# Attention on one core: the exponentials on VectorE as three half-float bit patterns, and 70 rows of them in place of 51

## The chip, the cores and the metric

The kernel runs on one core of one Trainium2 chip. Its time is the device time of one execution in microseconds. The profile is one execution, taken instruction by instruction; its span reaches from the first to the last instruction. TensorE does the matmuls, VectorE (DVE), ScalarE (ACT) and GpSimd (POOL) the elementwise work, SyncE (SP) issues most transfers.

## The reference

One multi-head attention layer with 16 heads of 28 columns, over 2048 positions of 448 columns, in bfloat16:

```python
qkv = (x @ wqkv).reshape(B, S, 3, H, Dh).transpose(2, 0, 3, 1, 4)   # B 1, S 2048, H 16, Dh 28
q, k, v = qkv
scores = einsum("bhqd,bhkd->bhqk", q, k) * Dh ** -0.5
o = einsum("bhqk,bhkd->bhqd", softmax(scores, -1), v)
return o.transpose(0, 2, 1, 3).reshape(B, S, D) @ wo
```

There are 16 × 2048 × 2048 = 67 million exponentials.

## The kernel before

**Units, rows and tiles.** The heads form four groups of four. A unit is one head group with one chunk of 512 queries: 16 units, counted from 0, four to a group (unit 12 is the first of the last group). A unit has 16 rows, one for each block of 128 keys, and a row has four tiles, one for each head: scores of 128 keys by 512 queries, one PSUM bank each. There are 256 rows and 1024 tiles. Rows are numbered through, so row 196 is row 4 of unit 12.

**Two ways to the exponentials.** Most rows go to ScalarE. A score group (`S`, line 864) puts two or three tiles into neighbouring banks of the five banks 0 to 4, and one activation (line 939) writes their exponentials to slots of `PT`, 36 slots of one tile each. Other rows, 51 of them, go to VectorE. Each of their tiles is computed alone (`SD`, also line 864), mostly beside a score group, in one of the `M` banks (5 to 7). Since the queries are scaled by 128 · log2(e), one instruction (line 886: a maximum and an addition) turns a score into the integer whose bits are about the bfloat16 number 2^z. When all four tiles stand in `DY`, four more instructions over the whole row (lines 896 to 902) make a power of two, `DS`, and a correction, `DU`. There are three buffers of each.

**Products with V.** TensorE multiplies the exponentials with V (`PV`, line 832), four heads side by side, into one `M` bank for a unit, in the order of the rows. Only a row's product frees its slots. A VectorE row needs three products: `DY` and `DS` with `V`, `DU` with `VK`, a weighted copy of V that GpSimd makes (line 577). A column of ones in V gives the sums for the softmax. At a unit's end VectorE copies the result out (line 731), the sums go through DRAM to be spread over the partitions (`scr_l`, `LT`, `scr_r`, `RB`, on SP's queue), and VectorE normalises (line 747). Units 12 to 15 finish the four query chunks, and behind each of them stand four output tiles: four matmuls each (line 718), one copy on VectorE (line 706) and one store. For the last unit the parts that don't need it (line 766) come ahead.

**What sets the order.** The transposes of x and the projections of Q, K and V stand among the units; those of later groups, and the output tiles, also need an `M` bank. A list scheduler with costs for each instruction fixes the order on every engine when the program is built. A planner chooses the VectorE rows ahead of it: it adds `rcost` to VectorE's account for each such row and `acost` to ScalarE's for each tile, and leaves at least `rgap` rows between two. `dlead` is how many tiles ahead of its place a row may start. Where the scheduler counts too little activity of TensorE, it puts in passes that multiply zeros (line 469).

```python
if t_d + CFG["rcost"] <= t_a + CFG["rlead"] and r < NROW - CFG["rend"] and gap >= CFG["rgap"]:
    t_d = max(t_d, t_a - 6.0) + CFG["rcost"]
    rows.append(r)
```

Of the kernel before, what the change touches and what calls it, by code (L numbers as in the profile page):

```python
# [334 lines left out]
CFG = {"late": 4.5, "load": 1.5, "load0": 18, "dcost": 2.3, "dlead": 32, "aslack": 250, "opp": 0.0, "oload": 2.5, "klead": 0.5, "vlag": 0.04, "hot1": 45000.0, "hotm": 3600.0, "nslack": 1300.0, "dlook": 20.0, "plook": 362.5, "rcost": 5.6, "rlead": 1.0, "rend": 4, "rgap": 2, "acost": 0.4455, "dprio": 0.0, "nride": 2}  # L335

PLAN = {
    "rows": None,
# [4 lines left out]
def _fast(nc, x, wqkv, wo, out, n_heads=16):  # L343
# [20 lines left out]
    QSCALE = 128.0 * LOG2E * scale  # L364
    ESCALE = 1.0 / (128.0 * LOG2E)
# [9 lines left out]
    P = _Prog()  # L375
    es = ExitStack()
    with es:
        def sb(name, shape, dt):
            return es.enter_context(nc.sbuf_tensor(name, shape, dt))
# [11 lines left out]
        VK = sb("VK", [128, NK, HC], BF16)  # L391
        DY = sb("DY", [128, NDR, 2048], I16)
        DS = sb("DS", [128, NDR, 2048], I16)
        DU = sb("DU", [128, NDR, 2048], FP16)
# [162 lines left out]
        v_ev = {}  # L557
        vk_ev = {}

        def proj_v(g, c, prio, early):  # L560
            mms = []
            for j in range(4):
                n = 4 * c + j

                def f(e, b, j=j, n=n):
                    ins = None
                    for it in range(NIT):
                        ins = e.matmul(ps[:, b * 512 + j * GD:b * 512 + (j + 1) * GD], xT[0:IT, it, n * 128:(n + 1) * 128],  # L568
                                       w_raw[0:IT, it, 2 * D + g * GD:2 * D + (g + 1) * GD], start=(it == 0), stop=(it == NIT - 1))
# [5 lines left out]
            vs = V[:, 4 * c:4 * c + 4, g * 128:(g + 1) * 128]  # L575
            vd = VK[:, 4 * c:4 * c + 4, g * 128:(g + 1) * 128]
            vk_ev[(g, c)] = P.add("pool", (lambda e: e.tensor_scalar(vd, vs, KAP, 1.0, ALU.mult, ALU.mult)), deps=[v_ev[(g, c)]],  # L577
                                  dur=1500, prio=prio, name=f"vk_{g}_{c}")


        for c in range(NCH):
# [231 lines left out]
        def pv(u, kt):  # L813
            g, c = units[u]
            r = u * NK + kt
            if r in n_row:
                ri = n_row[r] % NDR
                terms = [(V, DY[:, ri, :].bitcast(BF16)), (V, DS[:, ri, :].bitcast(BF16)), (VK, DU[:, ri, :].bitcast(BF16))]
                parts = [(w_, [t_[:, h * 512:(h + 1) * 512] for h in range(4)]) for w_, t_ in terms]
                deps_of = [row_ops[r], [row_ev[r][0]], [row_ev[r][1], vk_ev[(g, kt // 4)]]]  # L820
                slots = []
            else:
                slots = [tile_slot[(u, kt, h)] for h in range(4)]
                parts = [(V, [PT[:, pi * 512:(pi + 1) * 512] for _, pi in slots])]
                deps_of = [list({id(tile_ev[(u, kt, h)]): tile_ev[(u, kt, h)] for h in range(4)}.values())]

            def f_pv(e, k, w_, p_):
                ins = None
                b = pv_open[u].banks[0]
                for h in range(4):  # L830
                    hh = 4 * g + h
                    ins = e.matmul(ps[32 * h:32 * h + 32, b * 512:(b + 1) * 512], w_[:, kt, hh * 32:(hh + 1) * 32],  # L832
                                   p_[h], start=(kt == 0 and k == 0), stop=(kt == NK - 1 and k == len(parts) - 1), tile_position=(0, 32 * h))
# [12 lines left out]
            if r in n_row:  # L846
                row_pv[n_row[r]] = op
            if kt == NK - 1:
                (last_unit if u == NU - 1 else post_unit)(u, op)

        last_pv = [None]
# [19 lines left out]
        def row_tile(r, h, ph, partner, p_pr):  # L871
            u, kt = r // NK, r % NK
            g, c = units[u]
            t = (u, kt, h)
            if r not in n_row:
                n_row[r] = len(n_row)
                row_ops[r] = []
            ri = n_row[r] % NDR
            old = row_pv.get(n_row[r] - NDR)
            assert n_row[r] < NDR or old is not None, "DVE rows too close"  # L880
            deps = [kq_ev[(0, g, c)], kq_ev[(1, g, kt // 4)]] + (early_ev if ph > 0 else []) + (mid_ev if ph == 2 else [])
            hold = []
# [3 lines left out]
            o1 = P.add("dve", (lambda e, ri=ri, h=h, s=s: e.tensor_scalar(DY[:, ri, h * 512:(h + 1) * 512], bank(s.banks[0]), ZLO, ZADD, ALU.max, ALU.add)),  # L886
                       deps=[s, old], dur=600, prio=-90.0, name=f"D1_{r}_{h}", rel=[(s, 0)])
# [7 lines left out]
            Gt = U.bitcast(I16)  # L895
            og = P.add("dve", (lambda e: e.tensor_scalar(Gt, Y, 0x7F, 0x3F80, ALU.bitwise_and, ALU.bitwise_or)),  # L896
                       deps=row_ops[r] + [old], dur=600, prio=pr, name=f"DG_{r}")
            os_ = P.add("dve", (lambda e: e.tensor_scalar(S_, Y, 0xFF80, None, ALU.bitwise_and)),  # L898
                        deps=row_ops[r] + [old], dur=600, prio=pr + 0.001, name=f"DS_{r}")
            ou = P.add("dve", (lambda e: e.tensor_tensor(U, Gt.bitcast(BF16), Gt.bitcast(BF16), ALU.mult)),  # L900
                       deps=[og], dur=1130, prio=pr + 0.002, name=f"DU_{r}")
            oa = P.add("dve", (lambda e: e.tensor_tensor(U.bitcast(BF16), Y.bitcast(BF16), U, ALU.mult)),  # L902
                       deps=[ou], dur=1130, prio=pr + 0.003, name=f"DA_{r}")
            row_ev[r] = [os_, oa]
            done.update(4 * r + j for j in range(4))

# [815 lines left out]
```

## Time and profile before

| | |
|---|---|
| device time, three runs | 398.53, 403.58 and 403.67 us, median 403.58 |
| span of the profiled execution | 406.7 us (no other time of this execution is shown) |
| busy: TensorE, ScalarE, VectorE, GpSimd | 386.9, 378.0, 371.8 and 16.8 us |
| mean granted TensorE clock | 0.970 of full speed |
| matmuls; of these with zeros | 4331; 928 |
| ScalarE's exponentials (line 939) | 335 instructions, 375.0 us |
| VectorE's rows (lines 886 and 896 to 902) | 204 and 4 × 51 instructions |

A line of a group gives the source line, the engine, the operation, the output and inputs by the program's names, their shapes and the count; then busy time in us, the mean of one in ns, the idle time of the engine just ahead of them, and what ended most of it. PEld is TensorE's loading of weights. Instructions of one engine may overlap a little, so a group's busy time can be less than its count times its mean.

### The profile page before, as it was taken

How to read it: one execution, taken by the hardware profiler on the slowest of the kernel's cores; microseconds unless marked ns; L12 is line 12 of the kernel's file. 1: busy time of each engine (PE TensorE's matmuls, PEld its weight loads, DVE VectorE, ACT ScalarE, POOL GpSimd, SP SyncE). 2: the span in 40 equal slices, each digit the busy share in tenths (PEclk: the TensorE clock that was granted, in tenths of full speed). 3: DMA queues.
4: the chain of work that ended last, by engine and by line, in shares of the span. 5: the costliest groups of instructions: out<-in, count | busy, mean ns of one | idle time of the engine just before them, and what ended most of it. 6: DMA issues, size and time to landing. Idle time of an engine off the chain costs nothing.

```text
span 406.7 us, 9742 instructions
## 1 busy us (share of the span) xinstructions
PE 386.9 (95%) x4331; PEld 123.9 (30%) x4331; DVE 371.8 (91%) x548; ACT 378.0 (93%) x339; POOL 16.8 (4%) x25
## 2 busy tenths in 40 slices
PE   8999999999999999999999899999999899999997
PEld 4433323322323332333322222222222212222223
DVE  6569978999999999999999999999999967899964
ACT  2999979999999999999999999999999967999983
POOL 3010000200001000020000000000000000000000
PEclk9999969999999999999999999999999957999999
DMA  8200000000000000000000000000000000110111
GB/s 259 81 2 2 13 19 3 29 0 19 12 3 29 3 28 2 23 8 4 29 1 30 5 26 6 4 27 2 27 3 29 2 23 6 36 38 14 41 59 59
DMA packets 12980, 10.26 MB, mean 25 GB/s; under 512 B 5064, under 2 KB 10952, under 8 KB 12932
## 3 DMA queue, kind: packets, MB, share of 16 engines
q1 hardware_dynamic: 12132, 8.92, 7.1%
q8 instruction: 35, 0.57, 0.6%
q10 hardware_dynamic: 800, 0.66, 0.5%
q14 instruction: 13, 0.11, 0.1%
HBM read 7.50 MB, written 2.08 MB: 24 GB/s over the span
## 4 chain that ended last, share of the span: by engine, by line
ACT 43%; DVE 34%; PE 19%; DMA 2%; issue 1%; SPq 0%
ACT PT L939 43%; DVE DY L886 11%; PE ps L864 7%; DVE DU L900 6%; DVE DU L902 5%; PE ps L832 5%; DVE DU L896 3%; DVE DS L898 3%; PE ps L469 3%; PE ps L718 2%; DMA LT<-scr_l 2%; PE ps L550 2%; DVE V L521 1%; DVE KT L521 1%; DVE QT L519 1%; DVE OTS L731 1%
## 5 line engine op out<-in xcount | busy, mean ns | idle before, releaser
L939 ACT ACTIVATE PT<-ps 128x1536 bf16<-128x1536 f32 (+1 forms) x335 | 375.0, 1317 | 14.6 <-PE ps L864 13.9
L864 PE MATMUL ps<-QT,KT 28*128 28x512 bf16 x1024 | 164.2, 393 | 12.6 <-ACT PT L939 8.4
L886 DVE TENSOR_SCALAR DY<-ps 128x512 int16<-128x512 f32 x204 | 132.7, 679 | 11.0 <-PE ps L864 10.8
L864 PEld LDWEIGHTS ps<-QT,KT 28*128 28x128 bf16 x1024 | 40.3, 91 | 153.8 <-ACT PT L939 101.1
L832 PE MATMUL ps<-PT,V 128*32 128x512 bf16 x820 | 80.2, 398 | 2.1 <-issue 1.2
L469 PE MATMUL ps<-ZM,ZW 128*32 128x512 bf16 x928 | 74.9, 399 | 1.2 <-DVE ZM L451 1.2
L902 DVE TENSOR_TENSOR DU<-DY,DU 128x2048 bf16<-128x2048 bf16 x51 | 61.9, 1213 | 0.1
L900 DVE TENSOR_TENSOR DU<-DU 128x2048 f16<-128x2048 bf16 x51 | 61.8, 1213 | 0.0
L896 DVE TENSOR_SCALAR DU<-DY 128x2048 int16<-128x2048 int16 x51 | 34.7, 680 | 0.3
L550 PE MATMUL ps<-xT,w_raw 112*32 112x512 bf16 x512 | 35.0, 388 | 0.0
L898 DVE TENSOR_SCALAR DS<-DY 128x2048 int16<-128x2048 int16 x51 | 34.6, 678 | 0.0
L832 PEld LDWEIGHTS ps<-PT,V 128*32 128x32 bf16 x820 | 19.7, 94 | 47.1 <-issue 41.1
L469 PEld LDWEIGHTS ps<-ZM,ZW 128*32 128x32 bf16 x928 | 21.1, 98 | 27.9 <-issue 18.0
L832 PE MATMUL ps<-DU,VK 128*32 128x512 bf16 x204 | 20.8, 397 | 0.0
L832 PE MATMUL ps<-DY,V 128*32 128x512 bf16 x204 | 20.8, 397 | 0.0
L832 PE MATMUL ps<-DS,V 128*32 128x512 bf16 x204 | 20.6, 394 | 0.0
L577 POOL TENSOR_SCALAR VK<-V 128x512 bf16<-128x512 bf16 x16 | 13.4, 837 | 171.6 <-DVE V L521 171.6
L568 PE MATMUL ps<-w_raw,xT 112*128 112x112 bf16 x256 | 16.6, 214 | 0.0
L550 PEld LDWEIGHTS ps<-xT,w_raw 112*32 112x32 bf16 x512 | 12.0, 97 | 13.6 <-issue 3.0
L521 DVE CAST KT<-ps 128x512 bf16<-128x512 f32 x16 | 10.9, 682 | 4.4 <-PE ps L550 4.4
L568 PEld LDWEIGHTS ps<-w_raw,xT 112*128 112x128 bf16 x256 | 13.0, 98 | 5.8 <-issue 4.7
L706 DVE CAST OUTS<-ps 128x448 bf16<-128x448 f32 x14 | 8.6, 620 | 5.0 <-PE ps L864 2.6
(50 smaller groups left out, 121.2 us busy)
## 6 DMA issues: line engine op xcount, KB each, us to landing
RB<-scr_r SPq DMA_DIRECT2D x15, 256.0 KB
out_dram<-OUTS SPq DMA_DIRECT2D x14, 112.0 KB, 1.7
XO<-in_x_dram SPq DMA_DIRECT2D x3, 448.0 KB, 6.8
w_raw<-in_wqkv_dram SPq DMA_DIRECT2D x2, 392.0 KB, 6.5
wop<-in_wo_dram SPq DMA_DIRECT2D x16, 24.5 KB
scr_l<-OTS SPq DMA_DIRECT2D x15, 8.0 KB
LT<-scr_l SPq DMA_DIRECT2D x15, 8.0 KB, 1.6
scr_r<-RS SPq DMA_DIRECT2D x15, 8.0 KB, 1.4
```

Source lines behind the costliest of these rows:

```text
L469: ins = e.matmul(ps[32 * h:32 * h + 32, b * 512:(b + 1) * 512], ZW[:, :], ZM[:, :], start=shut, stop=shut, skip_group_check=not shut, tile ...
L521: fe = (lambda e: e.tensor_copy(evac[0](), evac[1](hold[0].banks[0])))
L550: ins = e.matmul(ps[32 * h:32 * h + 32, b * 512:(b + 1) * 512], w_raw[0:IT, it, col:col + 32], xT[0:IT, it, c * 512:(c + 1) * 512], start= ...
L568: ins = e.matmul(ps[:, b * 512 + j * GD:b * 512 + (j + 1) * GD], xT[0:IT, it, n * 128:(n + 1) * 128], w_raw[0:IT, it, 2 * D + g * GD:2 * D ...
L832: ins = e.matmul(ps[32 * h:32 * h + 32, b * 512:(b + 1) * 512], w_[:, kt, hh * 32:(hh + 1) * 32], p_[h], start=(kt == 0 and k == 0), stop= ...
L864: ins = e.matmul(bank(b), KT[32 * h:32 * h + rows, g, kt * 128:(kt + 1) * 128], QT[32 * h:32 * h + rows, g, c * QCH:(c + 1) * QCH], start= ...
L886: o1 = P.add("dve", (lambda e, ri=ri, h=h, s=s: e.tensor_scalar(DY[:, ri, h * 512:(h + 1) * 512], bank(s.banks[0]), ZLO, ZADD, ALU.max, AL ...
L896: og = P.add("dve", (lambda e: e.tensor_scalar(Gt, Y, 0x7F, 0x3F80, ALU.bitwise_and, ALU.bitwise_or)), deps=row_ops[r] + [old], dur=600, p ...
L898: os_ = P.add("dve", (lambda e: e.tensor_scalar(S_, Y, 0xFF80, None, ALU.bitwise_and)), deps=row_ops[r] + [old], dur=600, prio=pr + 0.001, ...
L900: ou = P.add("dve", (lambda e: e.tensor_tensor(U, Gt.bitcast(BF16), Gt.bitcast(BF16), ALU.mult)), deps=[og], dur=1130, prio=pr + 0.002, na ...
L902: oa = P.add("dve", (lambda e: e.tensor_tensor(U.bitcast(BF16), Y.bitcast(BF16), U, ALU.mult)), deps=[ou], dur=1130, prio=pr + 0.003, name ...
L939: ex = P.add("act", (lambda e, p0=p0, w=w, bf=bf: e.activation(PT[:, p0 * 512:(p0 + w) * 512], bank(bf(), w), AF.Exp, scale=ESCALE)), deps ...
```

## The change

The bit pattern becomes that of a half-float: queries are scaled by 1024 · log2(e), and the integer in `DY` is read as a half-float. The two other terms are the same integer plus 342 and plus 683, a third and two thirds of 1024, which moves z by 1/3 and 2/3. Each is multiplied with its own weighted copy of V (0.793 and 0.629). So `DS` and `DU` take one integer addition each in place of four instructions for a row. The copies, `VK1` and `VK2`, hold two head groups and are made on VectorE: for group 0 after each chunk of V, for the others once, after the last chunk, and for groups 2 and 3 after the last product of the group two before. `PT` has 30 slots, not 36; the row buffers are four, not three; `rcost` is 3.6, not 5.6, and `dlead` 24, not 32. With that the planner picks 70 rows.

```diff
-KAP = 0.1669921875
-ZLO = -64.0 * 128.0
-ZADD = 127.0 * 128.0 - 128.0 * 1.115731919743946
+HB = 1024.0
+SH1, SH2 = 342, 683
+KAP1, KAP2 = 0.79296875, 0.62890625
+ZADD = HB * (15.0 - 1.6415719559093558)
+ZLO = -ZADD
...
-    NPT = 36
-    NDR = 3
+    NPT = 30
+    NDR = 4
...
-            vk_ev[(g, c)] = P.add("pool", (lambda e: e.tensor_scalar(vd, vs, KAP, 1.0, ALU.mult, ALU.mult)), deps=[v_ev[(g, c)]],
-                                  dur=1500, prio=prio, name=f"vk_{g}_{c}")
+            if g == 0 or c == NCH - 1:
...
+                    op = P.add("dve", (lambda e, vd=vd, vs=vs, w_=w_: e.tensor_scalar(vd, vs, w_, None, ALU.mult)), deps=evs,
...
-                terms = [(V, DY[:, ri, :].bitcast(BF16)), (V, DS[:, ri, :].bitcast(BF16)), (VK, DU[:, ri, :].bitcast(BF16))]
+                terms = [(None, DY[:, ri, :].bitcast(FP16)), (VK1, DS[:, ri, :].bitcast(FP16)), (VK2, DU[:, ri, :].bitcast(FP16))]
...
+                        if g_ == g + 2 and op not in o_.deps:
+                            o_.deps.append(op)
...
-            og = P.add("dve", (lambda e: e.tensor_scalar(Gt, Y, 0x7F, 0x3F80, ALU.bitwise_and, ALU.bitwise_or)),
-            os_ = P.add("dve", (lambda e: e.tensor_scalar(S_, Y, 0xFF80, None, ALU.bitwise_and)),
-            ou = P.add("dve", (lambda e: e.tensor_tensor(U, Gt.bitcast(BF16), Gt.bitcast(BF16), ALU.mult)),
-            oa = P.add("dve", (lambda e: e.tensor_tensor(U.bitcast(BF16), Y.bitcast(BF16), U, ALU.mult)),
+            os_ = P.add("dve", (lambda e: e.tensor_scalar(S_, Y, SH1, None, ALU.add)),
+            oa = P.add("dve", (lambda e: e.tensor_scalar(U, Y, SH2, None, ALU.add)),
```

The lines of the changed program stand some places lower: the exponentials are at 947, scores at 877, tiles to integers at 899, the two additions at 908 and 910, products with V at 841, zeros at 472, copies of V at 584, projections at 553 and 571, output tiles at 727 and 775.

First place: VectorE around the tiles of unit 2, where rows follow each other. Before, the work of one row (line 886 to 902) with three tiles of the next among it and, at L731 and L521, other copies:

```order
L886 TENSOR_SCALAR DY<-ps 128x512 x4
L896 TENSOR_SCALAR DU<-DY 128x2048
L886 TENSOR_SCALAR DY<-ps 128x512
L898 TENSOR_SCALAR DS<-DY 128x2048
L886 TENSOR_SCALAR DY<-ps 128x512 x2
L731 COPY OTS<-ps 128x512
L886 TENSOR_SCALAR DY<-ps 128x512
L900 TENSOR_TENSOR DU<-DU 128x2048
L521 CAST V<-ps 128x4x4x28
L902 TENSOR_TENSOR DU<-DY,DU 128x2048
```

And after:

```order
L899 TENSOR_SCALAR DY<-ps 128x512 x2
L908 TENSOR_SCALAR DS<-DY 128x2048
L899 TENSOR_SCALAR DY<-ps 128x512 x2
L910 TENSOR_SCALAR DU<-DY 128x2048
L899 TENSOR_SCALAR DY<-ps 128x512 x2
L740 COPY OTS<-ps 128x512
L908 TENSOR_SCALAR DS<-DY 128x2048
L910 TENSOR_SCALAR DU<-DY 128x2048
```

Between two rows' tiles stand two instructions over 128x2048, not four, and none of them is a product of two tiles.

Second place: TensorE at the start of unit 12, around the first VectorE row of that unit. Before, V's projections have long been done, and the three products of the row (`DY`, `DS`, `DU`) stand together:

```order
L864 MATMUL ps<-QT,KT 128x512 x5
L832 MATMUL ps<-PT,V 32x512 x4
L864 MATMUL ps<-QT,KT 128x512 x2
L832 MATMUL ps<-DY,V 32x512 x4
L832 MATMUL ps<-DS,V 32x512 x4
L832 MATMUL ps<-DU,VK 32x512 x4
L469 MATMUL ps<-ZM,ZW 32x512 x4
```

After, the last projections of K (553) and V (571) stand between the row's first and second product, with zeros where a product could have stood:

```order
L841 MATMUL ps<-DY,V 32x512 x4
L877 MATMUL ps<-QT,KT 128x512 x5
...
L877 MATMUL ps<-QT,KT 128x512
L553 MATMUL ps<-xT,w_raw 32x512 x16
L877 MATMUL ps<-QT,KT 128x512 x5
L571 MATMUL ps<-w_raw,xT 128x112 x16
L877 MATMUL ps<-QT,KT 128x512 x4
L472 MATMUL ps<-ZM,ZW 32x512 x4
L877 MATMUL ps<-QT,KT 128x512 x3
L472 MATMUL ps<-ZM,ZW 32x512 x8
L841 MATMUL ps<-DS,VK 32x512 x4
```

The second product moved behind the copies of the whole group's V, and eight score groups lie between the two.

Third place: TensorE behind the last score group (the last row of line 864 or 877), up to the sums of the last unit (785; 794). Before:

```order
L864 MATMUL ps<-QT,KT 128x512 x2
L832 MATMUL ps<-PT,V 32x512 x12
L766 MATMUL ps<-wop,XO 128x448 x2
L832 MATMUL ps<-PT,V 32x512 x4
L766 MATMUL ps<-wop,XO 128x448 x3
L785 MATMUL ps<-SEL,OTS 128x4 x4
```

After, the first and the last rows of a longer stretch:

```order
L877 MATMUL ps<-QT,KT 128x512 x4
L841 MATMUL ps<-DS,VK 32x512 x4
L841 MATMUL ps<-DU,VK 32x512 x4
L841 MATMUL ps<-PT,V 32x512 x4
L727 MATMUL ps<-wop,XO 128x448 x4
L841 MATMUL ps<-PT,V 32x512 x4
L775 MATMUL ps<-wop,XO 128x448 x6
L727 MATMUL ps<-wop,XO 128x448 x2
...
L841 MATMUL ps<-DU,VK 32x512 x4
L841 MATMUL ps<-PT,V 32x512 x20
L794 MATMUL ps<-SEL,OTS 128x4 x4
```

Twelve of the last unit's sixteen rows now have products behind the last score group, and so have four output tiles.

More of the change, by code (lines that the diff above doesn't have):

```diff
@@ L390, in _fast @@
         PT = sb("PT", [128, NPT * 512], BF16)
-        VK = sb("VK", [128, NK, HC], BF16)
+        VK1 = sb("VK1", [128, 2, NK, 128], BF16)
+        VK2 = sb("VK2", [128, 2, NK, 128], BF16)
         DY = sb("DY", [128, NDR, 2048], I16)
         DS = sb("DS", [128, NDR, 2048], I16)
-        DU = sb("DU", [128, NDR, 2048], FP16)
+        DU = sb("DU", [128, NDR, 2048], I16)
         OTS = sb("OTS", [128, 2, 512], FP32)
@@ L574, in proj_v @@
                                ((lambda: Vd), (lambda b: bank(b)[:, 0:4 * GD].rearrange("p (n h d) -> p n h d", n=4, d=DH)), ms_v1), early, evac_dur=600)
[L575 to L578 removed]
+            if g == 0 or c == NCH - 1:
+                n0 = 4 * c if g == 0 else 0
+                vs = V[:, n0:4 * c + 4, g * 128:(g + 1) * 128]
+                evs = [v_ev[(g, cc)] for cc in range(n0 // 4, c + 1)]
+                for k_, (VK_, w_) in enumerate(((VK1, KAP1), (VK2, KAP2))):
+                    vd = VK_[:, g % 2, n0:4 * c + 4, :]
+                    op = P.add("dve", (lambda e, vd=vd, vs=vs, w_=w_: e.tensor_scalar(vd, vs, w_, None, ALU.mult)), deps=evs,
+                               dur=200 if g == 0 else 600, prio=prio + 0.01, name=f"vk{k_}_{g}_{c}")
+                    for cc in range(n0 // 4, c + 1):
+                        vk_ev[(g, cc, k_)] = op
         for c in range(NCH):
@@ L817, in pv @@
                 ri = n_row[r] % NDR
-                terms = [(V, DY[:, ri, :].bitcast(BF16)), (V, DS[:, ri, :].bitcast(BF16)), (VK, DU[:, ri, :].bitcast(BF16))]
-                parts = [(w_, [t_[:, h * 512:(h + 1) * 512] for h in range(4)]) for w_, t_ in terms]
-                deps_of = [row_ops[r], [row_ev[r][0]], [row_ev[r][1], vk_ev[(g, kt // 4)]]]
+                terms = [(None, DY[:, ri, :].bitcast(FP16)), (VK1, DS[:, ri, :].bitcast(FP16)), (VK2, DU[:, ri, :].bitcast(FP16))]
+                parts = [((lambda h, w_=w_: V[:, kt, (4 * g + h) * 32:(4 * g + h + 1) * 32] if w_ is None else w_[:, g % 2, kt, h * 32:(h + 1) * 32]),
+                          [t_[:, h * 512:(h + 1) * 512] for h in range(4)]) for w_, t_ in terms]
+                deps_of = [row_ops[r], [row_ev[r][0], vk_ev[(g, kt // 4, 0)]], [row_ev[r][1], vk_ev[(g, kt // 4, 1)]]]
                 slots = []
@@ L823, in pv @@
                 slots = [tile_slot[(u, kt, h)] for h in range(4)]
-                parts = [(V, [PT[:, pi * 512:(pi + 1) * 512] for _, pi in slots])]
+                parts = [((lambda h: V[:, kt, (4 * g + h) * 32:(4 * g + h + 1) * 32]), [PT[:, pi * 512:(pi + 1) * 512] for _, pi in slots])]
                 deps_of = [list({id(tile_ev[(u, kt, h)]): tile_ev[(u, kt, h)] for h in range(4)}.values())]
@@ L848, in pv @@
             if kt == NK - 1:
+                if c == NCH - 1:
+                    for (g_, _, _), o_ in vk_ev.items():
+                        if g_ == g + 2 and op not in o_.deps:
+                            o_.deps.append(op)
                 (last_unit if u == NU - 1 else post_unit)(u, op)
```

16 lines of the change are left out of this document (6 added, 10 removed).

## Prediction

> **What bounds the kernel now.** I read the busy row first, then the groups, then the idle time of ScalarE in order of time, and last the windows in which the TensorE clock fell.
>
> ```profile
> span 406.7 us, 9742 instructions
> PE 386.9 (95%) x4331; PEld 123.9 (30%) x4331; DVE 371.8 (91%) x548; ACT 378.0 (93%) x339; POOL 16.8 (4%) x25
> ACT 43%; DVE 34%; PE 19%; DMA 2%; issue 1%; SPq 0%
> L939 ACT ACTIVATE PT<-ps 128x1536 bf16<-128x1536 f32 (+1 forms) x335 | 375.0, 1317 | 14.6 <-PE ps L864 13.9
> L469 PE MATMUL ps<-ZM,ZW 128*32 128x512 bf16 x928 | 74.9, 399 | 1.2 <-DVE ZM L451 1.2
> ```
>
> ScalarE has one kind of work, the exponentials of L939, and it is idle for only 14.6 us between them, 13.9 of these for the score matmuls of L864. VectorE is as full (371.8 us). The chain that ended last swaps between the two. TensorE's 95% is no third bound: 928 of its matmuls multiply zeros (L469) and are put in only to keep it active. So an exponential taken off ScalarE brings time only if VectorE takes it at a lower price than now.
>
> Where ScalarE starts, runs gaplessly and ends (start, length, count):
>
> ```profile
> 9.82 25.77 ACT L939 ACTIVATE PT<-ps 128x1024 bf16<-128x1024 f32 x28 [0.63 <-PE ps L864]
> 232.23 92.77 ACT L939 ACTIVATE PT<-ps 128x1536 bf16<-128x1536 f32 x82 [0.31 <-PE ps L864]
> 335.99 2.53 ACT L939 ACTIVATE PT<-ps 128x1536 bf16<-128x1536 f32 x2 [0.91 <-PE ps L864]
> 340.28 15.92 ACT L939 ACTIVATE PT<-ps 128x1536 bf16<-128x1536 f32 x14 [1.76 <-PE ps L864]
> 391.93 6.95 ACT L939 ACTIVATE PT<-ps 128x1536 bf16<-128x1536 f32 x7 [1.12 <-PE ps L864]
> ```
>
> 28 exponentials of two banks take 25.77 us, 0.920 each. The 82 in the middle are three and two banks in turn: 41 pairs of 2.263, so three banks take 1.343. The last ends at 398.9, which leaves 7.8 us to the end of the span. Much of the idle time lies where the granted clock was half (columns: window, its length, then PE, PEld, DVE, ACT and POOL busy, PEclk):
>
> ```profile
> 51.00:57.80 6.80, 6.80 (x53) 1.25 (x45) 4.38 (x7) 4.87 (x5) 0.00 (x0) 0.50 0.07 26
> 232.00:324.00 92.00, 85.77 (x1031) 23.91 (x1028) 91.59 (x130) 91.77 (x82) 0.00 (x0) 1.00 0.05 14
> 324.00:341.00 17.00, 16.87 (x114) 3.42 (x118) 11.72 (x16) 11.39 (x11) 0.00 (x0) 0.50 0.06 18
> ```
>
> At full clock ScalarE works 91.77 of 92 us; at half clock it idles 5.6 of 17.0 (the waits of 0.91 and 1.76 for scores are among them) and 1.9 of 6.8: 7.5 us in all. That fits the runs: the profiled execution (406.7) lies 3.1 over the median of 403.6 and 8.2 over the fastest, 398.5. I make the sum against 406.7 and take 3.1 off at the end, which assumes that the clock falls about as often as now.
>
> **The change, part by part.** *ScalarE.* 19 more rows of 4 tiles leave it, 76 of 820 tiles. From the order of both programs: 152 groups of three banks become 137, 181 of two become 166, two single ones become one. At the durations above that is 371.9 before (the row says 375.0) and 337.4 after: **−34.5 us**, to about 340.5.
>
> *VectorE.* Its rows:
>
> ```profile
> L886 DVE TENSOR_SCALAR DY<-ps 128x512 int16<-128x512 f32 x204 | 132.7, 679 | 11.0 <-PE ps L864 10.8
> L902 DVE TENSOR_TENSOR DU<-DY,DU 128x2048 bf16<-128x2048 bf16 x51 | 61.9, 1213 | 0.1
> L900 DVE TENSOR_TENSOR DU<-DU 128x2048 f16<-128x2048 bf16 x51 | 61.8, 1213 | 0.0
> L896 DVE TENSOR_SCALAR DU<-DY 128x2048 int16<-128x2048 int16 x51 | 34.7, 680 | 0.3
> L898 DVE TENSOR_SCALAR DS<-DY 128x2048 int16<-128x2048 int16 x51 | 34.6, 678 | 0.0
> 153.14 1.28 DVE L886 TENSOR_SCALAR DY<-ps 128x512 int16<-128x512 f32 x2
> ```
>
> Neighbours overlap by 0.08 us: two L886 take 1.28, so the second adds 0.60 beside a duration of 0.68. Taken so, a row costs now 4 × 0.60 + 2 × 0.60 + 2 × 1.13 = 5.86, and afterwards, if an int16 addition costs what the int16 masks of L896 and L898 cost, 6 × 0.60 = 3.60. That is 51 × 5.86 = 299 against 70 × 3.60 = 252, −47. The weighted copies of V come from GpSimd to VectorE: six over 128x2048 at 0.60, and eight over 128x512, which no row shows on VectorE; between a quarter of that (0.15) and L886 (0.60) I take 0.3, and get +6. VectorE falls to 371.8 − 47 + 6 = 331: below ScalarE, so its saving is no gain of its own. The removed GpSimd copies had cover:
>
> ```profile
> L577 POOL TENSOR_SCALAR VK<-V 128x512 bf16<-128x512 bf16 x16 | 13.4, 837 | 171.6 <-DVE V L521 171.6
> ```
>
> An engine that waits 171.6 us and works 13.4 sets nothing; I count 0. But the copies now wait for the whole V of their head group. In unit 12 the second term of row 2 stands eight score groups behind the first, with every later product of the unit behind it; meanwhile ScalarE fills some 20 of the 30 slots in 8 × 1.13 = 9 us and is not held. In the order, all exponential groups but two of the last three find the products that free their slots issued before the next score group; so fewer slots (30 for 36), four buffers for three and the later start of rows cost 0 up to the end.
>
> The addition itself is the one unknown that matters. Same tiles, types and shape as L898, other arithmetic: the low end is 0.60; nothing makes it cheaper. The high end is one element at a time: L886 does 512 in about 0.53 beyond its fixed part, so 2048 take about 2.2. I take 0.60, by the nearest row.
>
> The Trainium skill speaks against it: "Advanced Engine Details and Errata", section "VectorE Performance Modes", lists BF16 and FP16 for the packed mode and not int16. By that sentence an int16 operation would get two elements a cycle, 1.13 us. This case's trace disagrees for the masks: int16 in 680 ns, against 1213 for the two-input product. The sum goes by the trace.
>
> *TensorE.* A pass (up to four matmuls side by side) follows a like one after 0.22 us; going between scores and anything else costs 0.1 more:
>
> ```profile
> 393.97 0.93 PE L718 MATMUL ps<-wop,XO 128*128 128x448 bf16 x4
> 394.83 0.39 PE L864 MATMUL ps<-QT,KT 28*128 28x512 bf16 x2
> 395.15 0.40 PE L832 MATMUL ps<-PT,V 128*32 128x512 bf16 x4
> 395.38 0.39 PE L832 MATMUL ps<-DY,V 128*32 128x512 bf16 x4
> 395.70 0.39 PE L864 MATMUL ps<-QT,KT 28*128 28x512 bf16 x3
> ```
>
> (395.15 to 395.38; 394.83 to 395.15. Four L718 and the switch take 0.86: 0.19 each.) Counted in the orders: score passes 419 then 472, since more single tiles of rows no longer ride beside a group; products with V 358 then 396; projections 128 and 144 small groups unchanged; switches 656 then 630. Useful TensorE time: 905 × 0.22 + 144 × 0.19 + 66 = 292 before, 996 × 0.22 + 27 + 63 = 309 after. Against ScalarE that is 78% and then 91%. The zero passes fall from 232 to 76. TensorE has little left to catch up with: over runs of eight score groups its work exceeds ScalarE's by up to 2 us in three stretches (around the starts of units 6 and 7, and in units 12 and 13, where the last projections now stand), by up to 0.8 before. ScalarE has up to 1.2 us of work in hand. I take **+3**, between 0 and the 6 of three full excesses. The half-float terms multiply a bf16 V; no row shows that pair. The low end is 0 (both are 16 bits as in the L832 rows), the high end is two passes for a mixed one: 210 × 0.22 = 46 us of TensorE. I take 0.
>
> *The end.* Behind the last score group stand before three products with V, two parts of the output projection and the last product: 1.6 us. After, 17 products with V stand there, 16 matmuls of the output projection and 12 of its parts, because the output tiles of units 12 to 14 come only when the rows give the M banks free: 17 × 0.22 + 28 × 0.19 + 0.8 of switches = 9.9. The last exponentials also wait for their slots: the one before the last needs the product of row 6 of the last unit, which now stands behind that group. What follows the last product is as now but for four parts already done:
>
> ```profile
> 384.63 0.55 SPq L745 DMA_DIRECT2D RB<-scr_r  x1
> 389.89 0.68 DVE L747 TENSOR_TENSOR XO<-RB,OTS 128x512 bf16<-128x512 f32 x1
> 398.93 0.40 PE L832 MATMUL ps<-PT,V 128*32 128x512 bf16 x4
> 402.43 0.92 PE L766 MATMUL ps<-wop,XO 128*128 128x448 bf16 x4
> 404.31 0.14 DVE L982 TENSOR_SCALAR FLAG<-ps 1x1 int32<-1x1 f32 x1
> ```
>
> From 398.93 to 406.7 are 7.8, less 0.6. So from the third last exponential group's release to the end 9.9 + 7.2 + 0.4 (output tile 8 waits for the normalised unit 14, whose broadcast now stands on SP behind the stores of tiles 0 to 2 and takes 5.3 us to its use, 384.63 to 389.89) = 17.5, where 7.8 follow now; 2.9 of exponentials lie inside. **+6.8.**
>
> Sum: 406.7 − 34.5 + 3 + 6.8 = 382.0 beside the profile; less 3.1, **379**.
>
> **The rivals.** *A, the additions are not at the masks' rate, and VectorE bounds (slower).* At L902's 1.13 they cost 140 × 0.53 = 74 more, VectorE 405; with the 34.9 us in which it idles now (406.7 − 371.8) 440, against the median 437. It turns at 331 + 140 × d = 371.8, an addition of 0.89 us. For it: no row shows an addition of integers. Against: two int16 rows at 680 and the copy of PSUM with an addition (L886) at no visible extra. One element at a time it would be 590. 6%.
>
> *B, waits for M banks come into the open.* Row tiles take a bank that VectorE must free:
>
> ```profile
> PEld ps L864 <- DVE DY L886: 19.2, 54, 0.8
> ```
>
> With 280 row tiles for 204 this is 26 us. Now it lies under ScalarE's work and beside zero passes. If half is exposed: 379 + 13 = 392 (12%); all, 405 (4%).
>
> *C, the clock.* Two thirds of the zero passes go, and half clock costs 5.6 us in 17. The 25 us of the gain are lost after 75 us more of it: 404. For it: 0.50 was granted where TensorE shows 16.87 busy of 17.00, so being busy did not protect it. Against: products with V, as active as zero passes, grow by 38, and the span they fill shrinks. 5%. The Trainium skill ("TensorE: Matmul & The Clock Gate", section "HAM oscillation — how this bites in real kernels") asks only that no idle gap exceeds about 3.4 us; by that nothing changes here, and the window 324 to 341 does not bear it out.
>
> *D, the mixed products take two passes:* TensorE 309 + 46 = 355, over ScalarE's 340.5 by 15: 394. Against: all L832 kinds, float or bit pattern, show 394 to 398 ns. 3%.
>
> **How the numbers follow.** The forecast, 368 to 388, has 68%: the low end is no clock loss at all (379 − 5) and half of the end's and stretches' cost back (−5), the high end the full 6 us of the stretches and one more slow window of 5.6. Under 368: 2%. B in half 12%, D 3%, B in full and C 9%, A 6%. The range leaves out the 2 below and, above 394, B in full, C and A with part of D: 368 to 394. Within 2% (395.5 to 411.7, about what a measurement of this kernel tells from no change) lie B in full and C: 9%. Slower is A: 6%. Faster is the rest, 85%.
>
> **What would show it.** Right: L908 and L910 at about 680 ns; 303 exponential groups at about 340 us; VectorE near 330 busy; L841 kinds all near 395 ns; ten or more us of TensorE behind the last score group; ScalarE idle 15 to 20 us, mostly near the starts of units 6 and 7, in units 12 and 13 and at the end. Wrong: additions of 1.1 us or more (A); long waits of L877 for L899 (B); PEclk at 5 in many slices (C); a mixed product longer than the others (D); or an end as short as now, which would put the time near 372.

## The result, and the profile after

The changed kernel took **386.3 us** in the median of six runs (380.3 to 396.0), the kernel before 401.7 in the six beside them (398.4 to 403.9): a ratio of **0.952, interval 0.943 to 0.961**. The runs of the changed kernel differ by how long TensorE was granted only half of its clock (mean clock 0.986 down to 0.935); the ratio takes the three of them at 0.973 and above (the medians alone give 0.962). The profiled execution is one of the long ones, 395.8 us. The page of the changed kernel, the rows that answer to those of before:

```profile
span 392.8 us, 8764 instructions
...
PE 375.7 (96%) x3854; PEld 118.5 (30%) x3854; DVE 335.5 (85%) x574; ACT 344.5 (88%) x308; POOL 3.4 (1%) x9
...
PEclk9999999999998799999998699999999997555999
...
ACT 51%; PE 33%; DMA 8%; DVE 6%; issue 1%; SPq 0%; ACTq 0%; DVEq 0%
...
L947 ACT ACTIVATE PT<-ps 128x1024 bf16<-128x1024 f32 (+1 forms) x304 | 341.6, 1284 | 28.9 <-PE ps L877 26.4
...
L841 PE MATMUL ps<-PT,V 128*32 128x512 bf16 x744 | 70.9, 405 | 2.3 <-issue 1.6
L908 DVE TENSOR_SCALAR DS<-DY 128x2048 int16<-128x2048 int16 x70 | 47.8, 682 | 0.9
L910 DVE TENSOR_SCALAR DU<-DY 128x2048 int16<-128x2048 int16 x70 | 47.6, 679 | 0.0
...
L841 PE MATMUL ps<-DU,VK 128*32 128x512 f16 x280 | 29.3, 409 | 0.0
```

VectorE has left the chain that ended last (34% before, 6% now); ScalarE and TensorE share it. ScalarE's own work fell by 33.5 us, but it now waits 28.9 us between exponentials where it waited 14.6. The windows say where (columns as before: PE, PEld, DVE, ACT, POOL, then the clock):

```profile
124.90:131.70 6.80, 6.80 (x50) 2.15 (x49) 5.16 (x9) 2.79 (x4) 0.00 (x0) 0.50 0.01 2
213.60:223.90 10.30, 10.30 (x79) 2.43 (x80) 7.55 (x13) 7.35 (x7) 0.00 (x0) 0.50 0.02 3
223.90:329.70 105.80, 101.31 (x1078) 30.71 (x1071) 99.54 (x167) 102.74 (x91) 0.00 (x0) 1.00 0.05 15
329.70:363.80 34.10, 34.10 (x228) 6.35 (x225) 23.11 (x37) 22.85 (x20) 0.00 (x0) 0.50 0.03 10
```

At half clock ScalarE is idle for 4.0 + 3.0 + 11.2 = 18.2 us of 51.2, 0.36 us for each us; it was 7.5 of 23.9 before (0.31). The end, in ScalarE's timeline (start, length, last bracket the idle time ahead and who ended it):

```profile
376.43 1.02 ACT L947 ACTIVATE PT<-ps 128x1024 bf16<-128x1024 f32 x1 [1.48 <-PE ps L841]
377.94 1.94 ACT L947 ACTIVATE PT<-ps 128x1536 bf16<-128x1536 f32 x2 [0.48 <-PE ps L841]
388.89 0.54 ACT L713 ACTIVATE OUTS<-ps 128x448 bf16<-128x448 f32 x1 [9.02 <-PE ps L818]
```

The last exponential ends at 379.9, 12.9 us ahead of the span's end (7.8 before), and the last two waits for slots stand ahead of it. So the 13.9 us by which the span fell are: −33.5 of ScalarE's work, +3.6 of idle time at full clock (6.5 to 10.1), **+10.7 of idle time at half clock**, +5.1 behind the last exponential, +0.2 at the start.

### The profile page after: what moved, and what is told of

Same layout as the page of the kernel before. It is cut to its first block, busy times and chain, and to the rows that moved or that the text cites. A ratio compares the mean times of both kernels' runs of the same rounds, so it can differ in the third digit from the quotient of the medians.

```text
span 392.8 us, 8764 instructions
## 1 busy us (share of the span) xinstructions
PE 375.7 (96%) x3854; PEld 118.5 (30%) x3854; DVE 335.5 (85%) x574; ACT 344.5 (88%) x308; POOL 3.4 (1%) x9
## 4 chain that ended last, share of the span: by engine, by line
ACT 51%; PE 33%; DMA 8%; DVE 6%; issue 1%; SPq 0%; ACTq 0%; DVEq 0%
ACT PT L947 51%; PE ps L877 12%; PE ps L841 10%; DMA RB<-scr_r 4%; PE ps L553 3%; PE ps L472 3%; DVE DY L899 3%; DMA scr_r<-RS 2%; DMA w_raw<-in_wqkv_dram 2%; PE ps L571 1%; PE ps L727 1%; DMA out_dram<-OUTS 1%; DVE XO L756 1%; PE ps L775 1%; DVE DS L908 0%
## 5 line engine op out<-in xcount | busy, mean ns | idle before, releaser
L947 ACT ACTIVATE PT<-ps 128x1024 bf16<-128x1024 f32 (+1 forms) x304 | 341.6, 1284 | 28.9 <-PE ps L877 26.4
L899 DVE TENSOR_SCALAR DY<-ps 128x512 int16<-128x512 f32 x280 | 183.0, 683 | 22.8 <-PE ps L877 18.9
L877 PE MATMUL ps<-QT,KT 28*128 28x512 bf16 x1024 | 176.5, 406 | 9.2 <-ACT PT L947 4.7
L908 DVE TENSOR_SCALAR DS<-DY 128x2048 int16<-128x2048 int16 x70 | 47.8, 682 | 0.9
L910 DVE TENSOR_SCALAR DU<-DY 128x2048 int16<-128x2048 int16 x70 | 47.6, 679 | 0.0
L472 PE MATMUL ps<-ZM,ZW 128*32 128x512 bf16 x304 | 28.9, 446 | 1.2 <-DVE ZM L454 1.2
L841 PE MATMUL ps<-DU,VK 128*32 128x512 f16 x280 | 29.3, 409 | 0.0
L841 PE MATMUL ps<-DY,V 128*32 128x512 f16 x280 | 29.3, 408 | 0.0
L841 PE MATMUL ps<-DS,VK 128*32 128x512 f16 x280 | 29.1, 406 | 0.0
L553 PEld LDWEIGHTS ps<-xT,w_raw 112*32 112x32 bf16 x512 | 11.2, 98 | 16.9 <-issue 4.3
L522 DVE TENSOR_SCALAR QT<-ps 128x512 bf16<-128x512 f32 x15 | 10.2, 684 | 3.9 <-PE ps L553 3.9
L756 DVE TENSOR_TENSOR XO<-RB,OTS 128x512 bf16<-128x512 f32 x15 | 10.2, 683 | 3.8 <-DMA RB<-scr_r 3.8
```

The costliest lines, as they stand in the source:

```text
L522: fe = (lambda e: e.tensor_scalar(evac[0](), evac[1](hold[0].banks[0]), mul, None, ALU.mult))
L756: nm = P.add("dve", (lambda e: e.tensor_tensor(OTN[:, g, c * QCH:(c + 1) * QCH], RB[:, ub, :], OTS[:, ub, :], ALU.mult)), deps=[l4] + list ...
L877: ins = e.matmul(bank(b), KT[32 * h:32 * h + rows, g, kt * 128:(kt + 1) * 128], QT[32 * h:32 * h + rows, g, c * QCH:(c + 1) * QCH], start= ...
L908: os_ = P.add("dve", (lambda e: e.tensor_scalar(S_, Y, SH1, None, ALU.add)), deps=row_ops[r] + [old], dur=600, prio=pr, name=f"DS_{r}")
L910: oa = P.add("dve", (lambda e: e.tensor_scalar(U, Y, SH2, None, ALU.add)), deps=row_ops[r] + [old], dur=600, prio=pr + 0.001, name=f"DU_{r}")
L947: ex = P.add("act", (lambda e, p0=p0, w=w, bf=bf: e.activation(PT[:, p0 * 512:(p0 + w) * 512], bank(bf(), w), AF.Exp, scale=ESCALE)), deps ...
```

## The experiments

Two theories were tried one after the other. What the expectations call theory 1 is the prediction's picture carried on: ScalarE bounds, TensorE has no reserve left, since 19 more rows took the place of 156 zero passes, and from that come the waits and the half clock. Theory 2 was formed when the first four runs and then the next four did not fit theory 1: half clock follows short stalls of TensorE, each with a cause of its own.

**The cheap terms without the rows.** The new bit patterns, but the old planner's 51 rows:

```diff
-"dlead": 24, "rcost": 3.6      NPT = 30   NDR = 4
+"dlead": 32, "rcost": 5.6      NPT = 36   NDR = 3
```

> The half-float method with 51 rows and the slots, buffers and planner numbers of before: VectorE loses 51 x 2.26 = 115 us of work, ScalarE keeps its 820 tiles. Theory 1 (ScalarE bounds, VectorE's saving is worth nothing until it takes rows over): ratio to before 0.99 to 1.01, VectorE busy near 265 us. Rival (the two take turns in the chain, which was on VectorE for 34% of its length, so cheaper rows bring time by themselves): 0.97 or less.

398.0 us (397.4 to 399.2), ratio 0.994 (0.987 to 1.001).

```profile
PE 371.6 (94%) x4367; PEld 121.4 (31%) x4367; DVE 276.0 (70%) x460; ACT 376.0 (95%) x339; POOL 3.4 (1%) x9
...
L947 ACT ACTIVATE PT<-ps 128x1536 bf16<-128x1536 f32 (+1 forms) x335 | 373.0, 1377 | 6.1 <-PE ps L877 5.8
```

VectorE's fall by nearly 100 us brought nothing: ScalarE bounds, and only the tiles that leave it count. No half clock lay between the exponentials of this execution.

**The end.** No VectorE row among the last six, in place of the last four (69 rows):

```diff
-"rend": 4
+"rend": 6
```

> The changed kernel, but no VectorE row among the last six rows (the planner's rend 6, not 4): 69 rows, and behind the last score group stand 2.7 us of TensorE, not 9.8. ScalarE gets one row back, +1.8 us. Theory 1: from the last exponential to the end about 8 us (12.9 in the changed kernel), so 3 to 5 us less in all at equal clock, near 377. Rival (the end hangs on the chain of the last unit's sums, not on the products in front of it): 1 to 2 us slower than the changed kernel.

384.2 us (382.9 to 405.3), ratio 0.958. In its profile 7.6 us follow the last exponential, not 12.9, but ScalarE waits 12.7 us at full clock, not 10.1, with 1.2 and 2.5 in the last stretch. At a clock of 0.973 its span is 380.9; two runs of the changed kernel at 0.973 have 380.2 and 381.3. So, with one row fewer, the end's work was only waited for earlier.

**More zeros, and fewer.** The scheduler's thresholds of activity, under which it puts in zero passes; 184 and 24 of them for 76:

```diff
-    FILL_MUST = 3750.0
-    FILL_HOT = 2787.5
+    FILL_MUST = 4200.0      # the other kernel: 2500.0
+    FILL_HOT = 3600.0       # the other kernel: 1500.0
```

> The changed kernel with the scheduler's floors of activity raised (3750 to 4200, 2787 to 3600): 184 passes of zeros, not 76. All passes together are then 361 us of TensorE by 0.22 us each, against 337 of exponentials. Theory 1 (the clock costs the time): mean granted clock 0.98 or more in every run, runs within 2% of each other, ScalarE's wait for scores at half clock gone; if TensorE then bounds at full clock, about 385, else 376. Rival (the waits come from the order and the M banks, the clock falls for other reasons): clock as low as now (0.935 to 0.986) and 390 or more.

> The changed kernel with the floors lowered (2500 and 1500): 24 passes of zeros, not 76; TensorE has 8.5 us less to do and 6.7 us, not 9.8, behind the last score group. Theory 1 (clock): half clock in more windows, mean clock under 0.93, 395 us or more. Rival (TensorE's work and order cost the time, the clock does not): 370 to 378.

With 184: 405.5 us (398.8 to 411.8), ratio 1.001. With 24: 384.6 (378.1 to 389.7), ratio 0.947. The kernel with 184, from its page:

```profile
L947 ACT ACTIVATE PT<-ps 128x1024 bf16<-128x1024 f32 (+1 forms) x304 | 342.8, 1249 | 41.5 <-PE ps L841 24.6
...
L472 PE MATMUL ps<-ZM,ZW 128*32 128x512 bf16 x736 | 61.1, 410 | 1.2 <-DVE ZM L454 1.2
```

ScalarE waits 41.5 us, most of it for products: zeros are no longer free (the one run at a clock of 1.0 took 398.8). Its clock, 0.963 to 1.0, was somewhat better than that of the changed kernel, but half clock still came, in two stretches of 10.2 us. With 24 zeros the clock was 0.933 to 0.977, no worse than with 76, and the time as in the changed kernel. So the number of zero passes does not decide the clock by itself.

**The changed kernel again, and 59 and 66 rows.**

```diff
-"rcost": 3.6, "rend": 4
+"rcost": 4.6, "rend": 4     # 59 rows
+"rcost": 3.9, "rend": 6     # 66 rows
```

> The changed kernel itself once more, unaltered, beside the next three on one chip. Theory 1 (TensorE has no reserve left, and the time moves with how long half clock is granted, about 0.36 us for each us of it): 379 to 397, spread over more than 6 us, each run within 3 us of 371 + 0.38 x its us at half clock (worked out from its mean clock). Rival (the time is set by waits for M banks or for slots, the clock has nothing to do with it): no relation between a run's clock and its time.

> One number altered: rcost 4.6 for 3.6, which makes it 59 rows of VectorE in place of 70. Counted in the order, 165 zero passes stand in it (76 with 70 rows), useful TensorE time by the prices of the prediction 286 us (309), ScalarE's exponentials 357 us (341). Theory 1: with the reserve back the granted clock stays at 0.98 or above in most runs, the runs lie within 4 us of each other, and the median is 384 to 388: half of the step from 51 rows to 70 is had for a third of TensorE's added work. Rival (each row is worth the same, 1.8 us of ScalarE, whatever the clock): the best run stands 20 us above that of the changed kernel, at about 400.

> Two numbers altered: rcost 3.9 for 3.6 and rend 6 for 4: 66 rows, none of them in the last six; 95 zero passes, useful TensorE time 301 us, exponentials 345 us, 1.5 us of products behind the last score group (9.9 in the changed kernel). Theory 1: best run 378 to 380, median 379 to 384, a spread below that of the changed kernel's 16 us, since 19 zero passes come back. Rival (every row left to VectorE counts, and the end's 5 us are only moved): 4 rows x 1.8 = 7 us slower than the changed kernel in the best run, 387.

The changed kernel: eleven runs from 378.4 us (clock 0.989) to 403.3 (0.913), which stand in the order of their clocks. Half clock is 2 × (1 − clock) of the span: 8 us in the shortest run and 70 in the longest, so 25 us for 62, 0.40 for each. The relation stands and its rival falls; the formula in the expectation lay 4 to 6 us too low, 2 of them because it had been made for the span. 59 rows: 392.8 us (391.1 to 398.3), between the two theories and as expected by neither.

66 rows: **369.6 us** (368.7 to 370.6), ratio **0.927 (0.924 to 0.930)**, 9 us under the best that either side had given, with four rows fewer on VectorE than in the changed kernel. Its page:

```profile
span 366.9 us, 8845 instructions
...
PE 351.7 (96%) x3904; PEld 114.4 (31%) x3904; DVE 321.6 (88%) x550; ACT 349.5 (95%) x315; POOL 3.4 (1%) x9
...
PEclk9999999999999999999999999999999999999999
...
L947 ACT ACTIVATE PT<-ps 128x1024 bf16<-128x1024 f32 (+2 forms) x311 | 346.5, 1291 | 3.7 <-PE ps L877 3.2
```

ScalarE has 6 us more work than with 70 rows, waits 3.7 us in all and never meets half clock. That is the version that beats both kernels. 19 more zero passes alone cannot be why, since 108 more (above) had not kept half clock away.

**Less work in TensorE, same order.** The product with `DS` covers 64 of 512 columns; the rest of that term is left out of the sum.

```diff
+                    wd = 64 if len(parts) == 3 and k == 1 else 512
-                                   p_[h], start=...
+                                   p_[h][:, 0:wd], start=...
```

> The order of the changed kernel, but the second product of each VectorE row (the one with DS) covers 64 of 512 columns; the rest of that term is left out of the sum. All waits, banks and slots stay; TensorE has 70 passes of some 0.03 us in place of 0.22, 13 us less work, and is that much less active. Theory 1: the time in which ScalarE is idle at full clock (10 us) falls by 3 or more, and a run at a clock of 0.973 takes 374 to 378 for 382; at a lower clock than now what is won goes back, half clock of 70 us (0.91) giving 390. Rival (waits for M banks or slots hold ScalarE, TensorE's fullness does not): full-clock idle as now, 381 at a clock of 0.973.

394.3 us (385.4 to 411.2), clock 0.960 down to 0.873. ScalarE's idle time at full clock was 9.7 us (10.8 in the run of the changed kernel beside it), so in this order TensorE's fullness is not what holds ScalarE there: theory 1's waits fell with this run. What it won it won at half clock: at 0.920 it took 396.1 us, the changed kernel 400.4 at 0.918. Its runs had on the whole more half clock than those of the changed kernel beside it (median clock 0.924 against 0.956), so the amount of TensorE's work may still bear on the clock.

**Where the clock falls.** The DMA queue, VectorE and TensorE in the changed kernel, ahead of the fall at 124.9:

```profile
115.28 0.33 SPq L752 DMA_DIRECT2D scr_r<-RS  x1
118.52 0.55 SPq L754 DMA_DIRECT2D RB<-scr_r  x1
```

```profile
120.47 1.34 DVE L899 TENSOR_SCALAR DY<-ps 128x512 int16<-128x512 f32 x2 [0.27 <-PE ps L877]
123.24 0.69 DVE L756 TENSOR_TENSOR XO<-RB,OTS 128x512 bf16<-128x512 f32 x1 [1.43 <-DMA RB<-scr_r]
123.84 1.28 DVE L899 TENSOR_SCALAR DY<-ps 128x512 int16<-128x512 f32 x2
```

```profile
123.00 0.39 PE L877 MATMUL ps<-QT,KT 28*128 28x512 bf16 x3
124.59 0.38 PE L877 MATMUL ps<-QT,KT 28*128 28x512 bf16 x1 [1.19 <-DVE DY L899]
```

Unit 3's normalisation (L756) stands at the head of VectorE's queue and waits 1.43 us for the broadcast of the sums. Behind it stand two tiles of rows (L899), and TensorE waits 1.19 us for the bank that the first of them would free. 0.3 us after that stall's end half clock sets in. Ahead of 213.6 another kind:

```profile
209.54 0.48 PE L877 MATMUL ps<-QT,KT 28*128 28x512 bf16 x3
211.63 0.61 PE L841 MATMUL ps<-PT,V 128*32 128x512 bf16 x8 [1.62 <-issue]
```

TensorE waits for nothing that the profile shows. At this place of its program a branch jumps over code that does not run in this case (`JUMP_AT`, in unit 8). Ahead of 329.7 VectorE waits 1.0 us for unit 12's broadcast, and TensorE 0.5:

```profile
327.63 0.69 DVE L756 TENSOR_TENSOR XO<-RB,OTS 128x512 bf16<-128x512 f32 x1 [1.00 <-DMA RB<-scr_r]
328.98 0.39 PE L877 MATMUL ps<-QT,KT 28*128 28x512 bf16 x1 [0.48 <-DVE DY L899]
```

In the kernel with 66 rows no stall of TensorE is longer than 0.4 between 10 us and 20 us ahead of the end, at the branch neither. From this came theory 2, and the last four runs. They ran on another chip than the runs before them, without the changed kernel and the one with 66 rows beside them; the kernel before took 399.9 us there, and 399.4 beside those two.

**The normalisations later.** Units 1, 3 and 12, three places later in VectorE's queue, once the order is made:

```diff
+        dv = P.order["dve"]
+        for u_, k_ in {1: 3, 3: 3, 12: 3}.items():
+            i = next(j for j, o in enumerate(dv) if o.name == f"NM{u_}")
+            dv.insert(i + k_, dv.pop(i))
```

> 70 rows as in the changed kernel; only the normalisations of units 1, 3 and 12 stand three places later in VectorE's queue, so that the broadcast of the sums has landed when VectorE comes to them. Theory 2 (half clock is granted behind stalls of TensorE of about 1 us; two of the three stalls come from VectorE waiting 0.9 to 1.6 us at the head of its queue for that broadcast, with TensorE waiting for a bank behind it): no wait of VectorE for RB over 0.3 us before unit 14, no half clock that begins near 125 or 328 us, mean clock 0.98 or more in most runs, median 376 to 381 where the changed kernel has 386 to 389. Rival (the activity of the passes alone sets the clock; the stalls are only its neighbours): clock and time spread as in the changed kernel, 378 to 403.

378.1 us (374.5 to 379.9), clock 0.982 to 1.0. In the profile no wait for a broadcast is left ahead of unit 14, and the only half clock between exponentials is that behind the branch (206.3, a stall of 1.36, then 13.7 us from 208.0). ScalarE's idle time at full clock stays (9.5 us, where the changed kernel had 10.1 and 10.8): what went is half clock.

```profile
span 377.8 us, 8764 instructions
...
PEclk9999999999999999999999579999999999999999
```

**The branch at the end of TensorE's program.**

```diff
-        P.HINT_AT = {"pe": "PV8_8", "dve": ...
-        P.JUMP_AT = {"pe": "PV8_11", "dve": ...
+        P.HINT_AT = {"dve": ...
+        P.JUMP_AT = {"dve": ...
```

> The changed kernel, but TensorE's branch over code that is never run here stands at the end of its program, not in unit 8. Theory 2: the stall of 1.4 to 1.6 us at 209 to 210 us goes, with 1 us of ScalarE's idle time there and the 10.2 us of half clock that set in behind it (3.6 us more); the best run is 374 to 376 (378.4), while half clock near 125 and 328 stays, and with it the spread. Rival: stall gone, half clock at 212 as now, 1 us won at most.

379.5 us (378.8 to 381.6), clock 0.985 to 0.989. The stall and the half clock behind it are gone; what is left is 6.8 us from 126.5, behind unit 3's wait. The best run is no better than that of the changed kernel (378.8 against 378.4), so the 374 to 376 that were expected did not come; but the long runs are gone, and the median is 10 us lower than that of the eleven runs. The 34 us stretch near 329 did not come either: unit 12 is reached earlier, and its normalisation does not wait there.

```profile
span 377.4 us, 8763 instructions
...
PEclk9999999999999799999999999999999999999999
```

The Trainium skill ("Runtime: NRT & Kernel Launch", section "Instruction fetch mechanics") says that a taken branch whose target is not in the fetched pages waits for the fetch. The stall of 1.62 us that went with the branch agrees; that it was the fetch itself no run here shows, and the kernel with 66 rows has the same branch without such a stall.

**Both.**

> The two edits together, 70 rows. Theory 2: no stall of TensorE over 0.7 us between 10 and 370 us, mean clock 0.99 or more in all runs, 371 to 376, the runs within 4 us of each other. That is 364.7 (exponentials 343.5, the start 10.3, the end 12.9 less 2 of overlap) + 7 to 10 of idle time at full clock. Rival: a spread of over 10 us as in the changed kernel.

376.2 us (375.0 to 377.1), ratio 0.939 (0.933 to 0.946), clock 0.994 to 1.0, runs within 2.1 us of each other. The same 70 rows, 76 zero passes and products as the changed kernel; four places of its program moved. One stretch of half clock is left between the exponentials, 3.4 us at 63.9, with no stall over 0.2 us just ahead of it.

```profile
span 375.3 us, 8763 instructions
...
L947 ACT ACTIVATE PT<-ps 128x1024 bf16<-128x1024 f32 (+1 forms) x304 | 339.6, 1293 | 12.5 <-PE ps L877 8.5
```

The kernel with 66 rows is still 8.4 us shorter (366.9): with 6.9 us more work on ScalarE it has 7.3 less idle time at full clock (2.9 for 10.2), 1.6 less at half clock, and 6.2 less behind the last exponential (7.7 for 13.9). So the clock is not all that it gains. It differs by `rcost` and by `rend`, and no run tells what each of them does.

**The converse.** The kernel with 66 rows, with the normalisations of units 3 and 7 five places earlier, that of unit 12 four:

```diff
+        for u_, k_ in {3: -5, 7: -5, 12: -4}.items():
```

> The converse, in the kernel with 66 rows (368.7 to 370.6 us, mean clock 0.995 to 1.0): the normalisations of units 3 and 7 stand five places earlier on VectorE, that of unit 12 four, so that VectorE waits for the broadcast some 1.4 us each time. Nothing else differs, no work is added. Theory 2: TensorE stalls by 1 us behind at least two of them, half clock of 3 us or more sets in within 4 us of such a stall, mean clock 0.985 or less, 373 to 385. Rival (waits without effect on the clock): at most the waits themselves, under 3 us, 369 to 372, mean clock 0.995 or more.

**390.3 us** (384.4 to 405.0), clock 0.969 to 0.902: 21 us lost by the place of three instructions. The waits came out at 2.2, 1.9 and 2.7 us, longer than meant. Around the first of them, VectorE, TensorE and then the windows of this kernel:

```profile
123.14 0.69 DVE L756 TENSOR_TENSOR XO<-RB,OTS 128x512 bf16<-128x512 f32 x1 [2.17 <-DMA RB<-scr_r]
```

```profile
124.49 1.03 PE L877 MATMUL ps<-QT,KT 28*128 28x512 bf16 x4 [2.37 <-DVE DY L899]
```

```profile
110.00:124.30 14.30, 11.94 (x141) 3.92 (x133) 10.52 (x18) 12.85 (x12) 0.00 (x0) 1.00 0.07 22
124.30:138.00 13.70, 13.51 (x97) 3.67 (x97) 8.41 (x14) 8.77 (x7) 0.00 (x0) 0.50 0.00 1
```

The kernel with 66 rows unaltered, same stretch:

```profile
124.30:138.00 13.70, 13.21 (x154) 4.84 (x154) 13.26 (x24) 13.43 (x12) 0.00 (x0) 1.00 0.01 2
```

Of the 15.7 us between the two spans (366.9, 382.6) 5.6 are idle time at full clock, at and around the stalls; 8.2 are idle time at half clock behind the first two. Behind the third (2.1 us, ended at 323.3) half clock did not set in.

Over the fourteen profiled executions there are 23 stalls of TensorE of 0.9 us or more between 10 us and 20 us ahead of the end. Half clock set in within 2.3 us of the end of 17. Of the six without, one is that third stall, and five are in the kernels with 51 and 59 rows (165 to 242 zero passes); with 184 zero passes and 70 rows two of two were followed. So how much TensorE has to do around a stall may decide what follows it; no run varied that alone. Of 28 stretches of half clock 11 had no such stall ahead of them, two long ones near 329 us among them (34 us in the changed kernel, behind a stall of 0.5; 37.5 us with the shortened product, behind none over 0.3). A stall is thus a strong cause, shown by taking it away and by putting it in, and not the only one. The place near 329 goes with unit 12's wait: three executions of this order had that wait (0.6 to 1.0 us) and half clock there, for 34, 3.4 and 37.5 us, and the three with a normalisation or the branch moved had neither. Why one stretch lasts 3.4 us and another 34 stays open.

## Why the prediction was right, and where it was off

379 us with 368 to 394 was forecast, and 386.3 measured. That it lies in the range owes something to luck: the range was made for other causes, the time of one execution hangs on how much half clock it gets, and the profiled one (395.8) lies outside. The sum was made for the span: 382.0 against 392.8, 10.8 too low. The 3.1 us taken off it set a span (406.7) against device times (403.6), and in every run here the device time is 1.7 to 3.1 us longer than the span of the same execution; so by these numbers some 5 would have been due (an estimate).

- **The additions** run at 682 and 679 ns (680 was taken), so rival A is out. The prediction took the Trainium skill's bracket "(BF16, FP16)" ("Advanced Engine Details and Errata", "VectorE Performance Modes") to leave int16 out, which would have meant 1.13 us; the table of that section asks only for a 16-bit type, and with that these rows agree.
- **ScalarE**: −33.5 for −34.5. **VectorE**: 335.5 busy for 331; a copy of V over 128x512 took 286 ns for the 0.3 taken between its bounds, one over 128x2048 682.
- **The mixed products** take 406 to 409 ns, those of two bf16 operands 405; at full clock one mixed pass starts 0.22 us after the other (208.99 and 209.21 us), as two of bf16 did in the kernel before (0.23; 395.15 and 395.38). Rival D is out.
- **The stretches**: idle time at full clock grew by 3.6, of which 2.0 are waits for slots at the end; so 1.6 for the 3 taken, with waits of 1.0 in unit 6 and of 1.0 and 1.5 in unit 12 (153.1, 281.4, 298.5 us) as the order had shown.
- **The end**: 5.1 more behind the last exponential, which with those 2.0 makes 7.1 for 6.8. Moving the rows away from the end brought nothing with 69 rows, though: there the end's work was waited for earlier. With 66 rows the end was short as well (7.7) and ScalarE did not wait for it.
- **Banks (B)**: waits for tiles of rows of 25.7 us, 63 times, for the 26 forecast. What mattered was less their sum than single ones such as that of 1.19 us, which stopped TensorE.

```profile
PEld ps L877 <- DVE DY L899: 25.7, 63, 1.5
```

- **The step that failed** is the last: "which assumes that the clock falls about as often as now". Idle time at half clock was 18.2 us for 7.5, and these 10.7 are nearly the whole miss: the errors of the other terms (+1.0 on ScalarE, −1.1 on the stretches and the end, +0.2 at the start) cancel. 11.2 of the 18.2 lie in the stretch at 329.7. With the stalls taken away (the run of both edits) the span was 375.3, of which 1.6 are idle time at half clock; the prediction's own sum without any half clock is 382.0 − 7.5 = 374.5.
- **Rival C** had the clock, and its price (5.6 in 17, 0.33 for each us; 0.36 measured), but as cause the lost zero passes, and that is at most a part of it: 184 of them cost more than they bought, and 66 rows with 95 kept the full clock until stalls were put in. The trace of before held a hint: a stall of 0.7 us of TensorE ends where the 17 us window at 324 begins. It did not hold the new wait: before, none of the 15 normalisations waited for its broadcast; now those of units 1, 3, 12 and 14 do.

## What to carry to other kernels

Where the order of in-order queues is fixed, look for an instruction that waits for a transfer at a queue's head, follow who waits behind it, and count not the wait but what its stall sets off: here three waits of 1.9 to 2.7 us cost 21. Before a kernel's variants are compared by one number, see whether their clocks agree; where runs spread by 20 us with the granted clock, as here, it is worth looking for what stands ahead of each fall: moving three instructions and a branch brought the median from 389.1 to 376.2, nearly as much as the change itself. The number of rows alone was a poor guide: best runs of 397, 391, 369, 383 and 378 us with 51, 59, 66, 69 and 70 of them.

## What was not expected of the hardware

- Half clock sets in behind stalls of TensorE of 0.9 to 2.4 us (17 of 23). The 28 stretches are 1 to 11 times 3.41 us long. The Trainium skill's rule ("TensorE: Matmul & The Clock Gate", "HAM oscillation — how this bites in real kernels") asks that no idle gap exceeds about 3.4 us; here shorter ones did it. Inside such a stretch TensorE shows no idle time (34.10 of 34.10) and still got half.
- Between the sums' small store (L752) and the issue of the broadcast behind it more time passes where a block of the program's code is being loaded. In the fourteen profiles 163 of 210 broadcasts were issued with no such block in flight since their store: 1.41 us behind it in the median. The other 47 overlapped one (16 KB in 0.9 to 1.7 us, or 8 KB): 3.0 in the median. In the 66-row kernel unit 3's escaped it:

```profile
116.83 0.33 SPq L752 DMA_DIRECT2D scr_r<-RS  x1
118.25 0.55 SPq L754 DMA_DIRECT2D RB<-scr_r  x1
```

  (1.42 us; 3.24 in the changed kernel, above.) That these 1.8 us are why unit 3 waits is read from the profiles; no run moved the code, and with 66 rows the normalisation itself also stands later in VectorE's queue (124.4 us, against 123.2).
